# Three edits at the end of a routed-expert kernel: scatters declared free of each other, the last tile's last two weight groups block by block, its last rows scaled by one operation

## The chip, the cores and the metric

The kernel runs on one core of one Trainium2 chip. The metric is the device time of one execution in microseconds. Engines are named as in the profile: PE is the matrix engine (PEld its weight loads), DVE the vector engine, ACT the scalar engine, POOL the GpSimd engine, SP the engine that issues most transfers. A trailing q (POOLq, SPq) marks rows of the engine's instruction queue: waits on semaphores, branches, register loads, drains.

## The reference, cut to what matters

Three layers follow each other. First a decaying linear attention (2 batches, 8 heads, 768 positions), whose output is laid out as 1536 tokens of 512 values. Then a dense two-layer network (512 to 2048 to 512) over all tokens. Then a mixture of 8 experts, of which each token uses one:

```python
expert_idx = np.argmax(logits, axis=1)
...
gate_w = probs[np.arange(N), expert_idx]
out = np.zeros((N, D), dtype=np.float32)
for e in range(E):
    mask = expert_idx == e
    h = np.maximum(x[mask] @ w1[e], 0.0)
    out[mask] = gate_w[mask, None] * (h @ w2[e])
```

Each of the 1536 rows of the result belongs to one token, hence to one expert, and is written once.

## The kernel before, in words

The dense layer and the experts are one list of `units`, one for each weight group. 24 units are the dense layer's (three chunks of four 128-token blocks, eight groups each). 16 units are the experts': four tiles of `WIDTH` 512, 384, 384 and 272 tokens, four groups each. Each tile holds tokens of one expert, chosen at run time. Tokens that don't fit go through a loop at the end (`tc.For_i`), which makes no pass with the inputs used here: each engine loads the loop's limit (L1050), branches past it (L1051), and meets the other engines in the closing rows, which carry L1126.

A tile (`Tile2`) is worked through like this. `gather` fetches its rows from a buffer in HBM and `gather_gate` the gates, by indirect transfers that POOL issues. `xprep` turns the rows. Then, for each group g, `l1` computes 256 hidden values for all tokens of the tile (24 matmuls), ACT and DVE write them as a rounded part `mh` and a remainder `ml`, and `l2` adds their product with the second weights to one accumulator for each block of 128 tokens: six matmuls for a block. In g = 3, the last group, `l2` also ends the block: ACT scales the accumulator by the gates into `osb` (L828), and POOL issues an indirect transfer that scatters these rows to the result `out` (L829). Blocks of a tile are numbered j; the last tile (272 tokens) has blocks of 128, 128 and 16.

The unit loop runs one unit ahead with `l1`: at step n it issues `l1` of unit n, and then `l2` of unit n-1 for all blocks. After the loop, `l2` of the last unit runs for all blocks. So PE's order at the end is: `l1` of the last unit, the last but one's `l2` for j = 0, 1, 2, the last one's `l2` for j = 0, 1, 2. The order on PE is the order of the program text. On the other engines a scheduler orders the instructions of the program and adds the waits that their data need; two scatters to `out` go to rows known at run time only, and the scheduler takes them as writes to the same tensor, one after the other.

For the last block of the last tile (16 tokens) the scaling is split by columns between ACT (L825) and DVE (L826). `osb` has four buffers.

Of the kernel before, what the change touches and what calls it, by code (L numbers as in the profile page):

```python
# [13 lines left out]
AF = mybir.ActivationFunctionType  # L14
ALU = mybir.AluOpType
# [3 lines left out]
NTOK = 1536  # L19
# [8 lines left out]
WIDTH = (512, 384, 384, 272)  # L28
QUARTERS = (4, 3, 3, 3)
NT = len(WIDTH)  # L30
ACC0 = (0, 0, 3, 2)
# [16 lines left out]
def kernel(  # L48
# [15 lines left out]
    V, A, G, PE, SP = nc.vector, nc.scalar, nc.gpsimd, nc.tensor, nc.sync  # L64
# [121 lines left out]
    NU = len(units)  # L186
# [561 lines left out]


    class Tile2:  # L750
        def __init__(self, e, ix, row, gx, gates, nt, nrow=NTOK, acc0=0, end=False):
            self.e, self.ix, self.row, self.gx, self.gates = e, ix, row, gx, gates
            self.nt, self.nrow, self.acc0, self.end = nt, nrow, acc0, end
            self.widths = [min(P, nt - P * j) for j in range((nt + P - 1) // P)]
            self.nb = len(self.widths)

# [51 lines left out]
        def l2(self, n, g, j):  # L808
            hi, lo = (x.rearrange("p (f d) -> p f d", f=2) for x in parts[2, n])
            gh, gl = act[n]  # L810
            w = self.widths[j]
            if g == 0:
                acc[self, j] = ps_acc.tile([P, DM], F32, name="m2a", tag=f"acc{(self.acc0 + j) % 4}")
            a = acc[self, j][0:w, :]
            sl = slice(j * P, j * P + w)
            for f in range(2):
                PE.matmul(a, lhsT=gh[:, f, sl], rhs=hi[:, f, :], start=(g == 0 and f == 0), stop=False)  # L817
                PE.matmul(a, lhsT=gh[:, f, sl], rhs=lo[:, f, :], start=False, stop=False)  # L818
                PE.matmul(a, lhsT=gl[:, f, sl], rhs=hi[:, f, :], start=False, stop=(g == 3 and f == 1))  # L819
            if g == 3:  # L820
                o = sb4.tile([P, DM], F32, name="osb", tag="x2s")
                gate = self.gate[0:w, j:j + 1]
                if self.end and j == self.nb - 1:

                    A.activation(o[0:w, 0:256], a[:, 0:256], AF.Copy, scale=gate)  # L825
                    V.tensor_scalar(o[0:w, 256:512], a[:, 256:512], gate, None, op0=ALU.mult)  # L826
                else:
                    A.activation(o[0:w, :], a, AF.Copy, scale=gate)  # L828
                G.indirect_dma_start(  # L829
                    out=out, out_offset=bass.IndirectOffsetOnAxis(ap=self.row[0:w, j:j + 1], axis=0),  # L830
                    in_=o[0:w, :], in_offset=None, bounds_check=NTOK - 1, oob_is_err=False,
                )


    at_tags.extend(([(ps_acc, f"acc{i}") for i in range(4)] + [(ps_at, "at")] * 2) * (NSTART + 1))
# [46 lines left out]
    def at(step, *fs):  # L882

        s0 = round(4 * step)
        for i, f in enumerate(fs):
            if f:
                plan.setdefault(s0 + i, []).append(f)
# [26 lines left out]
    def chunk_routed(c):  # L914
        rt["cnt"] = route_a(c)
        if first_blk[c] + CHUNKS[c] == EARLY:
            at(now[0] + 1.0, early_tile())
        if c == len(CHUNKS) - 1:
            ei, rt["next"] = route_next(rt["cnt"])
            e = SP.value_load(ei[0:1, 0:1], min_val=0, max_val=NE - 1)  # L920
            ix = small([P, QUARTERS[1]], "ixn", I32)
            tiles.append(Tile2(e, ix, None, None, gate_f, WIDTH[1], acc0=ACC0[1]))
            row_gates(EARLY, NBLK)
            A.dma_start(out=gate_f.rearrange("(p m) o -> p (m o)", m=NBLK), in_=gts)
            eis, rt["others"] = route_rest()
            rt["es"] = eis
# [8 lines left out]
    def other_rows():  # L935
        n = rt["rest"] + 2 * TMAX
        pt = rt["others"]()
        ix = small([P, n], "ixr", I32)
        V.tensor_copy(ix, pt)
        last = rt["rest"] - 1  # L940
        V.tensor_scalar(ix[:, last:last + 1], pt[:, last:last + 1], rt["fit"][:, 0:1], None, op0=ALU.mult)
        row, gx = places(ix, n, NBLK, "r")
        rt["tables"] = tuple(x[:, rt["rest"]:] for x in (ix, row, gx))
        c0 = 0
        for t in range(2, NT):
            e = SP.value_load(rt["es"][t - 2][0:1, 0:1], min_val=0, max_val=NE - 1)
            sl = slice(c0, c0 + QUARTERS[t])
            tiles.append(Tile2(e, ix[:, sl], row[:, sl], gx[:, sl], gate_f, WIDTH[t], acc0=ACC0[t], end=(t == NT - 1)))
            c0 += QUARTERS[t]

    def m2_l2(n, j):
        _, t, g = units[n]
        tiles[t].l2(n, g, j)
        if j == tiles[t].nb - 1:
            parts.pop((2, n))
            act.pop(n)

    for n in range(NU):
        lay, c, g = units[n]
        if lay == 1 and g == 0:  # L960
            if c + 1 < len(CHUNKS):
                m0 = first_blk[c + 1]
                fs = [f for m in range(max(m0, NSTART), m0 + CHUNKS[c + 1]) for f in pcs[m]]
                spread(fs, n + SPREAD[0], n + SPREAD[1])
            if c == 1:
                setup_routing()
        load_w(1, n + 2)
        load_w(2, n + 1)
        if n > K0:
            with tc.issue_after(last.ins):  # L970
                prep_w(1, n + 1)
                prep_w(2, n)
        else:
            with ExitStack() as after:
                if n == 0:

                    after.enter_context(tc.issue_after(ast[CHUNKS[0] - 1, "xl"].ins))
                    after.enter_context(tc.issue_after(whi[1, 0].ins))
                elif n == 1:
                    after.enter_context(tc.issue_after(squared[0, 1].ins))  # L980
                prep_w(1, n + 1)
                if n:
                    prep_w(2, n)
        if lay == 1:
            for f in range(2):
                done = m1_l1(n, f)
                if n == 0 and f == 1:

                    with tc.issue_after(done.ins), tc.issue_after(squared[0, 1].ins):
                        prep_w(2, 0)  # L990
                place(n, f)
                if n == N1 - 1:
                    tiles[0].xprep(2 * f)
                    tiles[0].xprep(2 * f + 1)
        else:
            if n == N1:

                last_scores = [m1_l2(n - 1, j) for j in range(CHUNKS[-1])]
            after_f = {
                N1: (((1, 0), (2, 0), (0, 0)), ((1, 1), (3, 0), (0, 1))),  # L1000
                N1 + 1: (((2, 1), (1, 2)), ((3, 1), (2, 2))),
            }.get(n, ((), ()))
            for f in range(2):
                last = tiles[c].l1(n, f)
                for m, i in after_f[f]:
                    last_scores[m][i]()
                if n == N1 + 2 and f == 1:
                    next_rows()
                if n == N1 + 3 and f == 0:
                    other_rows()  # L1010
                if c and c + 1 < NT and g == 0 and f == 0:
                    tiles[c + 1].gather()
                    tiles[c + 1].gather_gate()
                if c == 0 and g == 3:
                    tiles[1].xprep(2 * f)
                    tiles[1].xprep(2 * f + 1)
                if c and c + 1 < NT and g >= 2:
                    tiles[c + 1].xprep(2 * (g - 2) + f)
        if n == 0:
            place(0, 2)  # L1020
            place(0, 3)
        if n >= 1:
            lay1, c1, g1 = units[n - 1]
            if lay1 == 1 and n < N1:
                pend = []
                for j in range(CHUNKS[c1]):
                    pend.append(m1_l2(n - 1, j))
                    if j % 2 == 1:
                        place(n, 2 + j // 2)
                if g1 == 7:  # L1030
                    for j, p_ in enumerate(pend):
                        at(n + 1 + X2STEP[c1] * j, lambda p_=p_: [f() for f in p_])
                    at(n + ROUTE[c1], lambda c=c1: chunk_routed(c))
            elif lay1 == 2:
                for j in range(tiles[c1].nb):
                    m2_l2(n - 1, j)
                    if n == N1 + 1 and j == 0:
                        last_scores[3][2]()
                    if n == N1 + 1 and j == 2:
                        chunk_routed(len(CHUNKS) - 1)  # L1040
    for j in range(tiles[-1].nb):
        m2_l2(NU - 1, j)

    assert not plan

# [85 lines left out]
```

## Time and profile before

| what | us |
|---|---|
| median of 3 runs | 480.46 (479.46 to 480.70) |
| the profiled execution's own time | 479.74 |
| its span in the trace | 477.9 |
| PE busy in the span | 464.0 (97%) |
| the end of the last matmul's row | 466.56 |

The span runs from the first to the last instruction in the trace; the profiled execution's own time holds 1.8 us more. Tables of windows give, for each stretch, the busy time of each engine with the number of instructions, then the granted share of PE's clock, the share of the DMA engines that was busy, and the GB/s moved.

### The profile page before, as it was taken

The numbers are of one execution on the slowest core, as the hardware profiler recorded it, in microseconds if no ns is written. First come the engines' busy times: TensorE is split into PE (matmuls) and PEld (weight loads), VectorE is DVE, ScalarE is ACT, GpSimd is POOL, SyncE is SP. The second block draws the span as 40 slices with busy tenths as digits, with TensorE's granted clock in tenths as the row PEclk, the third lists the DMA queues.
The fourth block names the chain that finished last, engine by engine and source line by source line (L and its number), as shares of the span: only waits on it lengthen the run. The fifth ranks groups of instructions, "written<-read, shape, count | busy, mean of one in ns | idle before, by whom it ended". The sixth has DMA issues, their size and how long they took to land. (4 is left out here: it accounts for less than half of the span.)

```text
span 477.9 us, 7360 instructions
## 1 busy us (share of the span) xinstructions
PE 464.0 (97%) x2713; PEld 377.7 (79%) x2713; DVE 328.0 (69%) x726; ACT 266.7 (56%) x403; POOL 81.3 (17%) x83
## 2 busy tenths in 40 slices
PE   8999999999999999999999999999999999999990
PEld 5875778878878787878888888887878998998870
DVE  6889979879399997464999785666874354444410
ACT  2388879868975455445756754667233435435320
POOL 4513210002003120000000007000164400400201
PEclk9999999999999999999999999999999999999996
DMA  8999987768564223221433235330456543543201
GB/s 336 423 408 375 394 310 254 291 243 253 195 218 171 95 89 133 87 84 64 163 123 98 89 100 188 104 138 1 175 179 197 177 162 103 188 141 111 87 1 48
DMA packets 22651, 83.65 MB, mean 175 GB/s; under 512 B 3595, under 2 KB 3595, under 8 KB 20564
## 3 DMA queue, kind: packets, MB, share of 16 engines
q1 hardware_dynamic: 15842, 65.04, 38.9%
q10 hardware_dynamic: 4322, 11.55, 6.2%
q0 software_dynamic: 2448, 6.56, 3.9%
q8 instruction: 22, 0.36, 0.3%
q14 instruction: 17, 0.14, 0.1%
HBM read 68.44 MB, written 14.73 MB: 174 GB/s over the span
## 5 line engine op out<-in xcount | busy, mean ns | idle before, releaser
L213 DVE TENSOR_TENSOR w2l<-rw,w2h 128x1024 fp32r<-128x1024 f32 x32 | 39.2, 1225 | 55.2 <-ACT w2h L212 55.1
L700 PE MATMUL l<-xh,w1h 128*128 128x512 f32 x192 | 75.3, 397 | 0.9 <-ACT w1h L212 0.6
L743 PE MATMUL acc<-w2h,gh 128*128 128x512 f32 x184 | 72.8, 396 | 0.0
L702 PE MATMUL l<-xl,w1h 128*128 128x512 f32 x184 | 71.7, 390 | 0.0
L703 PE MATMUL l<-xh,w1l 128*128 128x512 f32 x184 | 71.7, 390 | 0.0
L745 PE MATMUL acc<-w2h,gl 128*128 128x512 f32 x184 | 71.7, 390 | 0.0
L744 PE MATMUL acc<-w2l,gh 128*128 128x512 f32 x184 | 71.7, 389 | 0.0
L212 ACT ACTIVATE w2h<-rw 128x1024 fp32r<-128x1024 f32 x32 | 33.9, 1059 | 57.1 <-PE m2a L819 30.0
L449 DVE CUSTOM_DVE_ANT_0 jk<-x2s,enb 128x512 f32<-128x512 f32 x72 | 48.0, 699 | 0.8 <-ACT x2s L434 0.6
L726 ACT ACTIVATE gh<-g_t 128x512 fp32r<-128x512 f32 x46 | 28.9, 629 | 33.0 <-DVE g_t L722 33.0
L213 DVE TENSOR_TENSOR w1l<-rw,w1h 128x1024 fp32r<-128x1024 f32 x32 | 39.7, 1241 | 11.1 <-ACT w1h L212 10.2
L719 ACT ACTIVATE r_t<-l,half 128x512 f32<-128x512 f32 x48 | 32.4, 680 | 26.2 <-PE l L703 25.8
L794 PE MATMUL m<-x2h,w1h 128*128 128x384 f32 (+2 forms) x128 | 43.9, 343 | 0.0
L700 PEld LDWEIGHTS l<-xh,w1h 128*128 128x128 f32 x192 | 35.8, 188 | 10.1 <-ACT w1h L212 1.2
L796 PE MATMUL m<-x2h,w1l 128*128 128x384 f32 (+2 forms) x128 | 43.3, 338 | 0.0
L795 PE MATMUL m<-x2l,w1h 128*128 128x384 f32 (+2 forms) x128 | 43.1, 337 | 0.0
L722 DVE SCALAR_TENSOR_TENSOR g_t<-r_t,l 128x512 f32<-128x512 f32 x46 | 31.4, 682 | 16.1 <-ACT r_t L720 16.0
L817 PE MATMUL m2a<-w2h,mh 128*128 128x512 f32 (+1 forms) x104 | 41.5, 399 | 0.0
L819 PE MATMUL m2a<-w2h,ml 128*128 128x512 f32 (+1 forms) x104 | 40.8, 392 | 0.0
L743 PEld LDWEIGHTS acc<-w2h,gh 128*128 128x128 f32 x184 | 34.5, 188 | 7.8 <-issue 0.5
L818 PE MATMUL m2a<-w2l,mh 128*128 128x512 f32 (+1 forms) x104 | 40.7, 391 | 0.0
L703 PEld LDWEIGHTS l<-xh,w1l 128*128 128x128 f32 x184 | 34.6, 188 | 7.2
(252 smaller groups left out, 843.9 us busy)
## 6 DMA issues: line engine op xcount, KB each, us to landing
rw<-wsc SPq DMA_DIRECT2D x32, 512.0 KB, 3.4
rw<-in_w_dram SPq DMA_DIRECT2D x32, 512.0 KB, 3.9
rw<-in_w_in_dram SPq DMA_DIRECT2D x8, 1024.0 KB
rw<-in_w_out_dram SPq DMA_DIRECT2D x8, 1024.0 KB, 12.8
wsc<-cw ACTq DMA_DIRECT2D x15, 512.0 KB, 6.8
qk_t<-in_qk_dram SPq DMA_DIRECT2D x12, 512.0 KB, 5.3
kv_t<-in_kv_dram SPq DMA_DIRECT2D x12, 512.0 KB, 12.5
x2d<-x2s ACTq DMA_DIRECT2D x12, 256.0 KB, 2.9
```

The costliest lines, as they stand in the source:

```text
L213: wlo[key] = eng.tensor_tensor(lo, r, hi.bitcast(F32), op=ALU.subtract)
L449: V.tensor_tensor_reduce(out=jk, in0=x2s, in1=enb[e // 2][:, e % 2, :], scale=1.0, scalar=0.0, op0=ALU.mult, op1=ALU.add, accum_out=lr[:, ...
L700: PE.matmul(pt, lhsT=hi[:, f, k, :], rhs=xh[c][:, k, :], start=(k == 0), stop=False)
L702: PE.matmul(pt, lhsT=hi[:, f, k, :], rhs=xl[c][:, k, :], start=False, stop=False)
L703: PE.matmul(pt, lhsT=lo[:, f, k, :], rhs=xh[c][:, k, :], start=False, stop=(k == 3))
L743: PE.matmul(a, lhsT=gh[:, f, sl], rhs=hi[:, f, :], start=(g == 0 and f == 0), stop=False)
L744: PE.matmul(a, lhsT=gh[:, f, sl], rhs=lo[:, f, :], start=False, stop=False)
L745: PE.matmul(a, lhsT=gl[:, f, sl], rhs=hi[:, f, :], start=False, stop=(g == 7 and f == 1))
L794: PE.matmul(pt, lhsT=hi[:, f, k, :], rhs=self.xh[:, k, :], start=(k == 0), stop=False)
L795: PE.matmul(pt, lhsT=hi[:, f, k, :], rhs=self.xl[:, k, :], start=False, stop=False)
L796: PE.matmul(pt, lhsT=lo[:, f, k, :], rhs=self.xh[:, k, :], start=False, stop=(k == 3))
L817: PE.matmul(a, lhsT=gh[:, f, sl], rhs=hi[:, f, :], start=(g == 0 and f == 0), stop=False)
```

## The change

Three things change, all in how the experts' results are finished.

1. Each scatter to `out` is put into one group, `rows_out`, and declared to have no dependency on the others in it.
2. At the last step of the unit loop, `l2` of the last two units runs block by block: unit NU-2 and unit NU-1 for j = 0, then both for j = 1, then both for j = 2. The loop behind it that ran the last unit is gone. `used` now releases the weights and activations of a unit.
3. The last block's 16 rows are scaled by one ACT operation over 512 columns, as those of all other blocks; the parameter `end` goes.

```diff
-    def __init__(self, e, ix, row, gx, gates, nt, nrow=NTOK, acc0=0, end=False):
+    def __init__(self, e, ix, row, gx, gates, nt, nrow=NTOK, acc0=0):
...
             if g == 3:
                 o = sb4.tile([P, DM], F32, name="osb", tag="x2s")
-                gate = self.gate[0:w, j:j + 1]
-                if self.end and j == self.nb - 1:
-
-                    A.activation(o[0:w, 0:256], a[:, 0:256], AF.Copy, scale=gate)
-                    V.tensor_scalar(o[0:w, 256:512], a[:, 256:512], gate, None, op0=ALU.mult)
-                else:
-                    A.activation(o[0:w, :], a, AF.Copy, scale=gate)
-                G.indirect_dma_start(
+                A.activation(o[0:w, :], a, AF.Copy, scale=self.gate[0:w, j:j + 1])
+                rows_out = G.indirect_dma_start(
                     out=out, out_offset=bass.IndirectOffsetOnAxis(ap=self.row[0:w, j:j + 1], axis=0),
                     in_=o[0:w, :], in_offset=None, bounds_check=NTOK - 1, oob_is_err=False,
                 )
+
+                tc.add_to_no_dep_group("rows_out", rows_out.ins)
+                tc.declare_no_dep(rows_out.ins, group="rows_out", reason="no two slots hold the same row")
...
     def m2_l2(n, j):
         _, t, g = units[n]
         tiles[t].l2(n, g, j)
-        if j == tiles[t].nb - 1:
-            parts.pop((2, n))
-            act.pop(n)
+
+    def used(n):
+        parts.pop((2, n))
+        act.pop(n)
...
+            elif n == NU - 1:
+
+                nb = tiles[c1].nb
+                for j in range(nb):
+                    m2_l2(n - 1, j)
+                    m2_l2(n, j)
+                used(n - 1)
+                used(n)
             elif lay1 == 2:
                 for j in range(tiles[c1].nb):
                     m2_l2(n - 1, j)
...
-    for j in range(tiles[-1].nb):
-        m2_l2(NU - 1, j)
+                used(n - 1)
```

## Rows read from the trace of the kernel before

**Rows 1.** The page's busy time, share of the span and instruction count of each engine

```profile
PE 464.0 (97%) x2713; PEld 377.7 (79%) x2713; DVE 328.0 (69%) x726; ACT 266.7 (56%) x403; POOL 81.3 (17%) x83
```

**Rows 2.** Busy time by stage: the experts' tiles, the last matmuls, and what follows them

```profile
core 0: us, PE busy (x) PEld busy (x) DVE busy (x) ACT busy (x) POOL busy (x), PEclk, DMA share, GB/s
...
400.00:462.00 62.00, 62.00 (x345) 54.18 (x344) 25.89 (x34) 25.13 (x39) 10.45 (x9) 1.00 0.34 111
462.00:466.56 4.56, 4.56 (x20) 2.81 (x18) 0.00 (x0) 1.38 (x2) 0.99 (x1) 1.00 0.07 27
466.56:477.94 11.38, 0.00 (x0) 0.00 (x0) 0.47 (x1) 0.47 (x1) 1.85 (x2) 0.58 0.11 41
```

**Rows 3.** Timeline from 462 us: start, duration, instruction, then idle before it and releaser

```profile
463.38 0.39 PE L819 MATMUL m2a<-w2h,ml 128*128 128x512 f32 x1
...
463.81 0.69 ACT L828 ACTIVATE osb<-m2a,gate 128x512 f32<-128x512 f32 x1 [5.16 <-PE m2a L819]
...
464.77 0.99 POOL L829 DMA_INDIRECT out_dram<-osb,rowr  x1 [14.64 <-ACT osb L828]
...
465.21 0.69 ACT L828 ACTIVATE osb<-m2a,gate 128x512 f32<-128x512 f32 x1 [0.71 <-PE m2a L819]
...
466.16 0.40 PE L819 MATMUL m2a<-w2h,ml 128*16 128x512 f32 x1
466.60 0.47 ACT L825 ACTIVATE osb<-m2a,gate 16x256 f32<-16x256 f32 x1 [0.70 <-PE m2a L819]
467.10 0.47 DVE L826 TENSOR_SCALAR osb<-m2a,gate 16x256 f32<-16x256 f32 x1 [7.97 <-ACT osb L825]
468.23 0.98 POOL L829 DMA_INDIRECT out_dram<-osb,rowr  x1 [2.47 <-ACTq L1051]
471.75 0.87 POOL L829 DMA_INDIRECT out_dram<-osb,rowr  x1 [2.54 <-issue]
```

**Rows 4.** Line 829 on POOL and its queue, 467 to 469 us: duration min/median/max

```profile
L829 POOLq EVENT_SEMAPHORE  x2: 2885/2895/2905, 464.6 to 468.1; - x2
```

**Rows 5.** Busy time in the microseconds in which the scatters' data move

```profile
466.00:467.00 1.00, 0.56 (x3) 0.03 (x1) 0.00 (x0) 0.40 (x1) 0.00 (x0) 1.00 0.64 262
469.00:470.00 1.00, 0.00 (x0) 0.00 (x0) 0.00 (x0) 0.00 (x0) 0.21 (x1) 0.50 0.23 94
470.00:471.00 1.00, 0.00 (x0) 0.00 (x0) 0.00 (x0) 0.00 (x0) 0.00 (x0) 0.50 0.42 168
473.00:474.00 1.00, 0.00 (x0) 0.00 (x0) 0.00 (x0) 0.00 (x0) 0.00 (x0) 0.50 0.13 31
```

**Rows 6.** Lines 1051 and 1126, the branch past the loop and the closing rows

```profile
L1051 POOLq INC_SWDGE_SEM  x1: 978/978/978, 472.5 to 472.5; - x1
...
L1126 POOLq DRAIN  x1: 3252/3252/3252, 473.5 to 473.5; - x1
...
L1126 SPq EVENT_SEMAPHORE  x2: 28/28/28, 473.9 to 474.0; - x2
```

**Rows 7.** Timeline of PE, ACT and DVE, 456 to 461 us

```profile
456.32 1.22 DVE L213 TENSOR_TENSOR w2l<-rw,w2h 128x1024 fp32r<-128x1024 f32 x1 [4.38 <-ACT w2h L212]
...
458.05 0.40 PE L817 MATMUL m2a<-w2h,mh 128*128 128x512 f32 x1
...
458.25 0.40 ACT L802 ACTIVATE mh<-m 128x272 fp32r<-128x272 f32 x1 [1.12 <-PE m L796]
...
458.68 0.44 DVE L803 SCALAR_TENSOR_TENSOR ml<-m,mh 128x272 fp32r<-128x272 f32 x1 [0.78 <-ACT mh L802]
...
459.67 0.40 PE L818 MATMUL m2a<-w2l,mh 128*128 128x512 f32 x1
...
460.60 0.40 PE L819 MATMUL m2a<-w2h,ml 128*128 128x512 f32 x1
```

**Rows 8.** Timeline of POOL, 355 to 360 us: gathers issued one behind the other

```profile
355.53 0.95 POOL L763 DMA_INDIRECT xg<-x2d,ixr  x1 [0.31 <-issue]
356.79 0.95 POOL L763 DMA_INDIRECT xg<-x2d,ixr  x1 [0.30 <-issue]
358.04 1.48 POOL L763 DMA_INDIRECT xg<-x2d,ixr  x1 [0.30 <-issue]
```

**Rows 9.** Waits from 300 us on: total us, times, longest

```profile
ACT w2h L212 <- PE m2a L819: 30.0, 10, 4.5
...
ACT osb L828 <- PE m2a L819: 10.6, 9, 5.2
```

More of the change, by code (lines that the diff above doesn't have):

```diff
@@ L750 @@
     class Tile2:
-        def __init__(self, e, ix, row, gx, gates, nt, nrow=NTOK, acc0=0, end=False):
+        def __init__(self, e, ix, row, gx, gates, nt, nrow=NTOK, acc0=0):
             self.e, self.ix, self.row, self.gx, self.gates = e, ix, row, gx, gates
-            self.nt, self.nrow, self.acc0, self.end = nt, nrow, acc0, end
+            self.nt, self.nrow, self.acc0 = nt, nrow, acc0
             self.widths = [min(P, nt - P * j) for j in range((nt + P - 1) // P)]
@@ L947, in other_rows @@
             sl = slice(c0, c0 + QUARTERS[t])
-            tiles.append(Tile2(e, ix[:, sl], row[:, sl], gx[:, sl], gate_f, WIDTH[t], acc0=ACC0[t], end=(t == NT - 1)))
+            tiles.append(Tile2(e, ix[:, sl], row[:, sl], gx[:, sl], gate_f, WIDTH[t], acc0=ACC0[t]))
             c0 += QUARTERS[t]
```

## The prediction, as made before the result

> **What bounds the kernel now.** I first read the page's busy times: PE works 464.0 us of the span, 97% [rows 1]. That says that the body is PE's and that a gain elsewhere must come from a stretch in which PE does nothing. The table by stage finds it [rows 2]: PE is busy 62.00 of 62.00 us from 400 to 462, 4.56 of 4.56 to the end of its last row at 466.56, and then 11.38 us follow in which no engine but POOL does more than half a microsecond. The timeline of the end shows what these are [rows 3]. The three scatters of the last tile start on POOL at 464.77, 468.23 and 471.75, though the rows of the second are scaled by 465.21 + 0.69 = 465.90 and those of the third by 467.10 + 0.47 = 467.57. The queue rows of the scatter line say why [rows 4]: two semaphore waits of 2.885 and 2.905 us begin at 464.6 and 468.1, so they end at 467.5 and 471.0, each some 0.75 us before the next scatter starts. The data of the scatters move between: 262 GB/s in the microsecond from 466, 94 and 168 in the two from 469 [rows 5]. So each scatter waits until the one before has landed. The names of releasers in [rows 3] (a branch on ACT's queue, "issue") are no help here: what is late is the landing.
>
> From the last scatter the end follows at a fixed distance. POOL runs an instruction of 0.978 us at 472.5 and a drain of 3.252 us at 473.5 that ends at about 476.79; SP's wait for the last landing is over by 473.9, and the span ends at 477.94 [rows 2, 6]. From the third scatter's start to the end that is 477.94 - 471.75 = 6.19 us.
>
> **The change, part by part.** The time is set by the third scatter's start plus 6.19, so each edit is priced by what it does to that start.
>
> *Scatters free of each other.* Nothing holds a scatter then but its own rows and POOL itself. The first scatter shows the step from rows to issue: ACT ends at 463.81 + 0.69 = 464.50, POOL starts at 464.77, 0.27 later [rows 3]. POOL itself can issue such transfers about 1.26 us apart: gathers without a wait between them stand 1.26 and 1.25 us apart, 0.30 idle [rows 8]. With the order on PE and the split as they are, the second scatter would start at 465.90 + 0.27 = 466.17 (POOL is free at 464.77 + 0.99 + 0.30 = 466.06), the third at 467.57 + 0.27 = 467.84: 3.91 us earlier than 471.75. This edit alone is nearly the whole gain.
>
> *The last two groups block by block.* No matmul is added or taken away. 36 matmuls run from 458.05 in steps of 0.23, six to a block and unit. Now block 0 ends with the 24th (row at 463.38), block 1 with the 30th, block 2 with the 36th (466.16). After the change block 0 ends with the 12th (the row at 460.60), block 1 with the 24th, block 2 with the 36th as before [rows 3, 7]. ACT starts the scaling 0.04 us after the last matmul's row ends, so block 0's `osb` is ready at 461.04 + 0.69 = 461.73 and its scatter starts at 462.00; block 1's takes block 0's present place, 464.77; block 2's is unchanged. With the waits gone, this edit is worth nothing in the end: block 2 still ends last. With the waits left in, it would be worth much (rival A). What it asks for earlier is the last unit's data: `w2l` in the eighth matmul (the row at 459.67) rather than the 20th, and it is ready at 456.32 + 1.22 = 457.54; the second half of `ml` in the 12th (460.60), and it is ready at 458.68 + 0.44 = 459.12 [rows 7]. Margins of 2.1 and 1.5 us hide it; if a margin were gone, PE would idle for what is missing, and the end would move by as much.
>
> *One operation for the last rows.* The two halves don't run side by side: DVE starts at 467.10, ACT ended at 467.07, and DVE's row names ACT as its releaser [rows 3]. One ACT operation of 16x512 isn't in the trace; it lies between 16x256 (0.47) and 128x512 (0.69). It has the columns of the second and the rows of the first. I take 0.69: with 16 rows half the columns still cost 0.47, so the rows aren't what ACT saves on, and the columns are those of the row of 0.69. Then `osb` is ready at 466.60 + 0.69 = 467.29 instead of 467.57, 0.28 earlier; at 0.47 it would be 0.50 earlier. Before the change this was hidden under the wait to 471.0; with the waits gone it counts in full.
> The Trainium skill ("ScalarE: Activation LUTs", What ACT_TABLE_LOAD costs) gives 186 ns and 0.833 ns a column, and 93 ns for each pointer operand, whatever the rows: an estimate of 0.71 us for 512 columns with the gate as pointer, which would make the gain 4.17 rather than 4.19. The row of 0.69 bears that out for 128 partitions; no row shows 16.
>
> *Sum.* The third scatter starts at 466.60 + 0.69 + 0.27 = 467.56; POOL has been free since 464.77 + 0.99 = 465.76. That is 4.19 us before 471.75. The three scatters then stand 2.78 and 2.79 apart, while the data of one move within about a microsecond [rows 5], so they don't meet.
>
> *The other ten scatters.* Those of the first three tiles are freed too, and the scheduler may place them and the gathers among them otherwise on POOL. Nothing on the path waits for them: in [rows 9] ACT's `osb` waits for PE's accumulator, not for a free buffer, and ACT's weight conversion waits for PE, not for a transfer; PE has no gap in 400 to 462. I cost them at nothing, hidden under PE. If that cover is gone, rival C says what it costs.
>
> **The numbers.** The span becomes 477.94 - 4.19 = 473.75, the profiled execution's own time 479.74 - 4.19 = 475.55, and the median 480.46 - 4.19 = 476.27, which I forecast as 476.3. The profiled execution lies 0.72 below the median of the runs.
>
> **The rivals.** *A. The waits stay.* The declaration may not take effect, or a wait on a reused semaphore may take the old one's place. Then the order on PE does the work: scatter 0 starts at 462.00, lands 2.73 later (464.77 to 467.5) at 464.73, scatter 1 starts 0.73 after that, 465.46, lands 2.77 later at 468.23, scatter 2 starts 0.75 later at 468.98. Gain 2.77, time 477.7. For it: only that the scheduler places the waits. Against it: gathers, which have nothing to wait for, show no such wait [rows 8].
>
> *B. Completions are served one after the other.* POOL's drain ends 2.89 us after SP saw the last landing (476.79 against 473.9) [rows 6]. If POOL spends that time on each transfer in turn, then scatter 0 (landed 464.73) is done at 467.62, scatter 1 (467.50) at 470.51, scatter 2 (467.56 + 2.15 = 469.71) at 473.40, and the end follows 1.15 later at 474.55. Gain 3.39, time 477.1. For it: nothing else in the rows explains a drain of 3.25 us. Against it: the present end fits a fixed distance just as well.
>
> *C. The scheduler's new order costs PE.* If in the first three tiles, with ten block ends, ACT's queue now takes an `osb` (0.69) ahead of an activation that PE waits for, each costs up to 0.69; four of them eat 2.8 and leave a gain of 1.4 or less. Against it: `osb` already waits for PE and has no reason to move; only POOL loses waits. Time about 479.1 to 480.5, no measurable change.
>
> *D. The other side: the drain pays for each scatter.* If the waits between scatters were where POOL finished the last transfer, and the drain now finishes all three, it costs 3 x 3.25 instead of 3.25. It would start 4.19 earlier, at 469.35, end at 479.10, and the span at 480.25: 2.31 longer, time 482.8. It decides once each added piece is over 2.1 us. Against it: between landing (467.5) and the next start (468.23) POOL needs only 0.73, and gathers in a row start 1.26 apart with no such block between them [rows 8]. For it: the row of an indirect transfer is short (0.87) beside the drain that follows.
> On that row the Trainium skill ("Perfetto Trace Analysis", DMA Instruction — SWDGE (GPSIMD)) says that the profiler's end is when the last descriptor is written, and that the core completes the instruction later; so hidden work on POOL behind the row is possible, and no row here shows how much.
>
> **Chances.** The forecast 0.74, A 0.07, B 0.08, C 0.06, D 0.05. About 0.3% (1.4 us) is what a measurement of this kernel can tell from no change. Forecast, A and B are faster: 0.89; C is the same: 0.06; D is slower: 0.05. The range runs from the lowest run less the gain, 479.46 - 4.19 = 475.3, less 0.2 for the cheaper ACT operation, 475.1, to A's 477.7 with 0.2 for the runs above their median, 477.9; it takes in B.
>
> **What the next profile should show.** Scatters of the last tile at about 462.0, 464.8 and 467.6, no semaphore wait of 2.9 us on POOL's queue in that stretch, one `osb` row of about 0.69 at 466.6 and none on DVE, PE's last row still ending at 466.56, a drain of about 3.25 from 469.3, and an end at 473.75. The prediction is wrong if PE's last row moves (order or readiness), if the scatters still stand 3.5 us apart (A), or if the drain is longer (B, D).

## The result, and the profile after

| | before | after |
|---|---|---|
| median us | 479.96 (479.33 to 480.70, 4 runs) | 475.23 (474.53 to 475.31, 4 runs) |
| ratio, 95% interval | | 0.9894 [0.9875, 0.9914] |
| span of the profiled execution | 477.94 | 472.65 |
| from the end of PE's last row to the end of the span | 11.38 | 6.28 |

The kernel is faster by 1.1%, about 5 us; 4.2 us were forecast. The interval of the timed runs is 4.1 to 6.0 us, so they alone don't rule out 4.2; it is the traces below that do. The table by stage of the changed kernel answers to [rows 2]. Its last stretch begins where PE's last row ends.

```profile
core 0: us, PE busy (x) PEld busy (x) DVE busy (x) ACT busy (x) POOL busy (x), PEclk, DMA share, GB/s
400.00:462.00 62.00, 62.00 (x344) 54.73 (x343) 25.67 (x34) 25.81 (x40) 9.87 (x10) 1.00 0.32 111
462.00:466.37 4.37, 4.37 (x19) 2.08 (x17) 0.00 (x0) 0.69 (x1) 1.77 (x2) 1.00 0.22 88
466.37:472.65 6.28, 0.00 (x1) 0.00 (x0) 0.00 (x0) 0.68 (x1) 0.87 (x1) 0.69 0.09 32
```

PE is as full as before, and only the stretch behind it shrank, from 11.38 to 6.28 us. The timeline of the end of the changed kernel answers to [rows 3] and [rows 7].

```profile
460.41 0.40 PE L819 MATMUL m2a<-w2h,ml 128*128 128x512 f32 x1
...
460.85 0.69 ACT L822 ACTIVATE osb<-m2a,gate 128x512 f32<-128x512 f32 x1 [2.39 <-PE m2a L819]
...
461.81 0.98 POOL L823 DMA_INDIRECT out_dram<-osb,rowr  x1 [19.17 <-ACT osb L822]
...
463.63 0.69 ACT L822 ACTIVATE osb<-m2a,gate 128x512 f32<-128x512 f32 x1 [2.10 <-PE m2a L819]
...
464.59 0.98 POOL L823 DMA_INDIRECT out_dram<-osb,rowr  x1 [1.80 <-ACT osb L822]
...
465.97 0.40 PE L819 MATMUL m2a<-w2h,ml 128*16 128x512 f32 x1
466.41 0.68 ACT L822 ACTIVATE osb<-m2a,gate 16x512 f32<-16x512 f32 x1 [2.09 <-PE m2a L819]
467.36 0.87 POOL L823 DMA_INDIRECT out_dram<-osb,rowr  x1 [1.79 <-ACT osb L822]
```

Each scatter now names ACT's `osb` as its releaser, starts 0.27 us after it, and stands 2.8 us from the next. The third starts 0.99 us after PE's last row (467.36 - 466.37); 1.00 was forecast. So far the steps held. The end is the surprise: 472.65 - 467.36 = 5.29 us behind the third scatter, where I had put 6.19. These are the rows of POOL's queue for the branch past the loop (L1056) and the closing drain (L1131), which answer to [rows 6]; start times are at the end of each row.

```profile
L1056 POOLq INC_SWDGE_SEM  x1: 951/951/951, 465.3 to 465.3; - x1
...
L1131 POOLq DRAIN  x1: 4363/4363/4363, 467.1 to 467.1; - x1
...
L823 POOLq MOVE  x2: 29/29/29, 461.6 to 466.3; - x2
```

The 0.95 us instruction of the branch, which stood behind the third scatter before (472.5 against 471.75), now runs at 465.3, two us ahead of it. The drain begins before the scatter does and ends at 471.5. The last row shown has the register moves of two scatters: the later one, at 466.3, is the third scatter's, and it stands right behind the branch's instruction, which ends at 466.29. The order of POOL's instructions in the program of the changed kernel says how that came about (its last rows, loop body left out; the row marked ISA is the 0.95 us instruction):

```
48 L823 DMA out_dram<-osb,rowr 1536x512 x5
49 L1055 TENSOR_LOAD lim
50 L1056 COMPARE_AND_BRANCH
...
63 L1056 ISA
64 L1056 UNCONDITIONAL_BRANCH
65 L823 DMA out_dram<-osb,rowr 1536x512
```

Before, all six scatters of the last two tiles stand ahead of the branch. Now five do, and the sixth, the last block's, stands behind the loop and its branch.

### The profile page after: what moved, and what is told of

It reads as the page before. It is cut to its first block, busy times and chain, and to the rows that moved or that the text cites. A ratio compares the mean times of both kernels' runs of the same rounds, so it can differ in the third digit from the quotient of the medians.

```text
span 472.7 us, 7356 instructions
## 1 busy us (share of the span) xinstructions
PE 463.7 (98%) x2713; PEld 377.7 (80%) x2713; DVE 326.7 (69%) x725; ACT 266.6 (56%) x403; POOL 82.4 (17%) x83
## 4 chain that ended last, share of the span: by engine, by line
PE 68%; issue 20%; POOL 6%; DVE 3%; ACT 1%; POOLq 0%; another core or an unknown queue 0%; ACTq 0%
PE l L700 10%; PE acc L743 9%; PE l L702 9%; PE acc L744 9%; PE l L703 9%; PE acc L745 9%; POOL out_dram L823 2%; PE ao L335 2%; PE sc L308 2%; POOL xg L763 2%; POOL gate L771 2%; PE acc L738 1%; PE ao L348 1%; PE as L377 1%; PE m L794 1%
## 5 line engine op out<-in xcount | busy, mean ns | idle before, releaser
L745 PEld LDWEIGHTS acc<-w2h,gl 128*128 128x128 f32 x184 | 34.5, 188 | 7.3
```

## The experiments

Two numbers of each trace are compared: the third scatter's start after the end of PE's last row, and the end of the span after that start. Their sum is free of what PE's part does from one execution to the next, which the last experiment shows to be more than some of the differences. Each line is one profiled execution. The page of the profile calls spans on POOL rough; the sum does not depend on them, the split into two columns does.

| run | third scatter after PE | end after it | sum | timed ratio, 95% |
|---|---|---|---|---|
| before | 5.19 | 6.19 | 11.38 | |
| one operation alone | 5.19 | 6.18 | 11.37 | 1.0002 [0.9982, 1.0023] |
| block order alone | 2.53 | 6.19 | 8.72 | 0.9943 [0.9926, 0.9961] |
| free alone | 2.41 | 5.29 | 7.70 | 0.9936 [0.9911, 0.9961] |
| free, one operation | 2.41 | 5.29 | 7.71 | 0.9914 [0.9892, 0.9935] |
| free but for the loop's, one operation | 0.99 | 6.44 | 7.43 | 0.9925 [0.9906, 0.9944] |
| changed, loop's scatters not free | 0.99 | 6.28 | 7.27 | 0.9906 [0.9884, 0.9927] |
| changed, memset behind | 0.99 | 5.95 | 6.94 | 0.9910 [0.9875, 0.9945] |
| free, block order | 1.28 | 5.30 | 6.58 | 0.9903 [0.9877, 0.9928] |
| changed | 0.99 | 5.29 | 6.28 | 0.9892 [0.9869, 0.9915] |

The line of the changed kernel is that of its second profile. The timed ratios have intervals of 0.8 to 1.7 us to each side; differences below that are read from the traces alone.

**The changed kernel again.** No edit.

> The changed kernel itself, again, as the measure for the three beside it. Theory P (POOL's order): because the loop's scatters are in the group too, the scheduler could put the last tile's third scatter behind the loop's branch on POOL, so that the branch and the 0.95 us instruction behind it run while POOL waits for rows; the time from the third scatter's start to the end of the span is then 5.3 us in place of 6.2. Theory L (landing): the order does not matter, the end follows the last landing or the rest of the earlier transfers' handling, which is shorter here by chance or because the scatters overlap. Both expect here what was measured once: about 4.7 to 5.1 us less than before, third scatter 1.28 us after the end of PE's last row minus 0.3, so about 1.0 us after it, and 5.3 us from there to the end.

Measured: 474.80 against 479.80 us; 0.99 and 5.29 us, as the first time. (The text's "1.28 minus 0.3" and "1.0" are the same figure, 0.99 here.)

**The changed kernel with the loop's scatters outside the group.** This decides between the two theories of the shorter tail.

```diff
+                if self.nt == 2 * P:
+                    return
                 tc.add_to_no_dep_group("rows_out", rows_out.ins)
                 tc.declare_no_dep(rows_out.ins, group="rows_out", reason="no two slots hold the same row")
```

(Only the loop's tiles have 2 x 128 tokens.)

> The changed kernel, but the two scatters in the loop (which makes no pass) are left out of the group, so the third scatter must stay ahead of the branch on POOL. Everything else is as in the changed kernel. Theory P: the 0.95 us instruction stands between the third scatter and the drain again, the tail is 6.2 us, and the time is 0.9 us longer than the changed kernel's. Theory L: the tail stays at 5.3 us and the time is the changed kernel's.

In the program's order all six scatters stand ahead of the branch again. The third scatter, the stretch behind PE's last row, and the rows of the branch (L1058) and the drain (L1133) on POOL's queue in this run:

```profile
466.93 0.87 POOL L823 DMA_INDIRECT out_dram<-osb,rowr  x1 [1.78 <-ACT osb L822]
...
465.94:473.21 7.27, 0.00 (x1) 0.00 (x0) 0.00 (x0) 0.68 (x1) 0.87 (x1) 0.68 0.08 28
...
L1058 POOLq INC_SWDGE_SEM  x1: 969/969/969, 467.7 to 467.7; - x1
...
L1133 POOLq DRAIN  x1: 3386/3386/3386, 469.0 to 469.0; - x1
```

The third scatter starts at 466.93, the instruction runs behind it, and the end comes 6.28 us after it instead of 5.29. The third scatter landed 2.15 us after its start in both runs (469.08 here, 469.51 in the changed kernel), so the landing does not account for the 0.99 us. Theory P holds, theory L falls. The pieces of the 6.28 are not quite those of the old 6.19: the drain ends 3.74 us after the branch's instruction, 3.28 before, and the span ends 0.82 us after the drain, 1.15 before; why stays open. The two timed ratios (0.9892 and 0.9906) lie in that order, but their intervals overlap.

**Scatters free, nothing else.**

```diff
-                G.indirect_dma_start(
+                rows_out = G.indirect_dma_start(
...
+                tc.add_to_no_dep_group("rows_out", rows_out.ins)
+                tc.declare_no_dep(rows_out.ins, group="rows_out", reason="no two slots hold the same row")
```

> The kernel before with the scatters declared free and nothing else: order on PE and split of the last rows as before. By my terms the third scatter starts 467.84 - 466.56 = 1.28 us after PE's last row ends, 3.91 us earlier than before. Theory P: the third scatter goes behind the branch here too, so the tail is 5.3 us and the gain is 3.91 + 0.91 = 4.8 us (ratio 0.990). Theory L without the new order of blocks: the three scatters stand 1.3 to 1.7 us apart, their handling overlaps, and the tail is 6.2 us or longer: gain 3.9 us or less (ratio 0.992).

The tail is 5.29, as theory P said. But the third scatter starts 2.41 us after PE's last row, not 1.28, and the gain is 3.68 us in the trace, near theory L's number for another reason. POOL's timeline and, from its queue, the row of the branch (L1054) and the third scatter's register move:

```profile
464.64 0.98 POOL L829 DMA_INDIRECT out_dram<-osb,rowr  x1 [21.95 <-ACT osb L828]
466.04 0.98 POOL L829 DMA_INDIRECT out_dram<-osb,rowr  x1 [0.42 <-ACT osb L828]
468.84 0.87 POOL L829 DMA_INDIRECT out_dram<-osb,rowr  x1 [1.81 <-DMA gate<-gate_f,gxr]
```

```profile
L1054 POOLq INC_SWDGE_SEM  x1: 951/951/951, 467.0 to 467.0; - x1
...
L829 POOLq MOVE  x1: 29/29/29, 468.0 to 468.0; - x1
```

The branch's instruction runs from 467.0 to 467.95, between the second and the third scatter, and the third, whose queue rows follow at 468.0, starts 0.89 after it; what fills the 0.89 us is not shown. The releaser that the row names, a gate's transfer, had landed long before; it is not what was late.

**Scatters free, one operation, old order on PE.** The edit above, and `end` never set.

> Scatters declared free and the last rows scaled by one operation, the order of blocks on PE as before. By my terms the block order adds nothing once the waits are gone: the same time as the changed kernel within 0.2 us, third scatter 1.0 us after PE's last row. If instead the spacing of the scatters counts (2.8 us apart in the changed kernel, 1.4 here), the tail here is longer than the changed kernel's 5.3 us by up to 1.4.

```profile
468.58 0.87 POOL L829 DMA_INDIRECT out_dram<-osb,rowr  x1 [1.82 <-DMA gate<-gate_f,gxr]
...
466.16:473.87 7.71, 0.01 (x1) 0.00 (x0) 0.00 (x0) 0.68 (x1) 1.47 (x2) 0.75 0.16 60
```

Measured 2.41 and 5.29: the rows were ready about 0.3 us earlier than in the run before and it changed nothing, so the rows aren't what the third scatter waits for. My first reading, that the block order adds nothing, is refuted: against the changed kernel it is worth 7.71 - 6.28 = 1.43 us in the traces (the timed intervals overlap).

**The same with the loop's scatters outside the group.** Both edits from above.

> Scatters declared free except the two in the loop, one operation for the last rows, the order of blocks on PE as before. In the run without the new block order the third scatter started 2.41 us after PE's last row, not 1.0. Theory P2: what held it was the branch with its 0.95 us instruction, now ahead of it on POOL right behind the second scatter. With the branch behind the third scatter again it must start 1.0 us after PE's last row, with a tail of 6.2 to 6.3, 7.3 us together, and be 0.4 us faster than with the branch ahead. Rival R2: scatters 1.4 us apart hold each other up (POOL or the transfers). Then the third starts at 2.4 us here too, and with the tail of 6.2 it ends 8.7 us after PE's last row.

ACT's and POOL's rows of this run, and the branch's (L1056):

```profile
468.86 0.68 ACT L828 ACTIVATE osb<-m2a,gate 16x512 f32<-16x512 f32 x1 [0.70 <-PE m2a L819]
```

```profile
467.03 0.98 POOL L829 DMA_INDIRECT out_dram<-osb,rowr  x1 [21.95 <-ACT osb L828]
468.43 0.98 POOL L829 DMA_INDIRECT out_dram<-osb,rowr  x1 [0.42 <-ACT osb L828]
469.81 0.87 POOL L829 DMA_INDIRECT out_dram<-osb,rowr  x1 [0.40 <-ACT osb L828]
...
L1056 POOLq INC_SWDGE_SEM  x1: 969/969/969, 470.7 to 470.7; - x1
```

With the branch behind it the third scatter starts 0.27 us after its rows again, though the scatters stand only 1.40 and 1.38 us apart. So P2 holds and R2 falls: what held the third scatter was the branch, not the spacing. What follows PE is 7.43 us against 7.71, somewhat less than the 0.4 expected, because the tail is 6.44 here. It is 0.16 us longer than with the scatters 2.8 us apart (6.28): the branch's instruction starts 0.91 us after the third scatter in place of 0.75, while the drain takes 3.39 us in both. So the spacing is not quite free, and why stays open. The timed ratios don't tell the two apart.

**Block order alone.** The edits of the unit loop and `used`, without the others.

> The kernel before with the last two weight groups block by block and nothing else; the scatters wait for each other. By rival A's terms: scatters 4.56 and 1.10 us before and 2.42 us after the end of PE's last row, 2.77 us earlier than before for the third, branch behind the third scatter, tail 6.2 us. Time about 2.8 us less than before (ratio 0.994). If the early use of the last unit's data made PE wait, PE's last row would end later instead.

```profile
461.33 0.98 POOL L829 DMA_INDIRECT out_dram<-osb,rowr  x1 [10.78 <-ACT osb L828]
464.90 0.98 POOL L829 DMA_INDIRECT out_dram<-osb,rowr  x1 [2.59 <-issue]
468.42 0.87 POOL L829 DMA_INDIRECT out_dram<-osb,rowr  x1 [2.54 <-DVEq L1059]
```

The first scatter starts as early as expected (4.56 before the end of PE's last row at 465.89), then each waits for the one before, 3.57 and 3.52 us apart. The gain is 11.38 - 8.72 = 2.66 us, 2.77 expected, and the tail is the old 6.19. PE's order has no wait in it: PE is busy without a gap from 360 to 465.89.

**One operation alone.** `end` never set.

> The kernel before with the last rows scaled by one ACT operation and nothing else. My term: the rows are ready 0.28 us earlier, but the third scatter waits for the second's landing some 4 us longer, so nothing is gained: third scatter 5.2 us after PE's last row, tail 6.2, ratio 1.000. If the wait were not the landing but the rows, the third scatter would start 0.28 us earlier.

Measured 5.19 and 6.18: hidden, as expected.

**Free and block order, split kept.**

> The changed kernel with the last rows split between ACT and DVE as before. My term for the one operation was 0.28 us: third scatter 1.27 us after PE's last row instead of 0.99, tail 5.3, 6.6 us together. If POOL's branch bounds the third scatter here as well, the split costs nothing and the sum is 6.3.

Measured 1.28 and 5.30, sum 6.58: the one operation is worth 0.30 us once nothing else holds the scatter.

**A memset behind the third scatter in the changed kernel.** It clears the attention's mask, which nothing reads by then.

```diff
+    rows_last = []
...
+                rows_last.append(rows_out)
...
+    with tc.issue_after(rows_last[-1].ins):
+        G.memset(dmask, 0.0)
```

> The changed kernel with one added memset of 128x1024 on POOL behind the third scatter (it clears a mask that nothing reads any more). Theory T1: the drain on POOL ends a fixed 3.26 us after POOL's last piece of work, so the end moves by about the memset's duration. Theory T2: the drain follows the last transfer (2.0 us after its landing in the changed kernel), and the memset runs in its shadow: no change if the memset takes less than 3 us.

```profile
467.51 0.87 POOL L824 DMA_INDIRECT out_dram<-osb,rowr  x1 [1.79 <-ACT osb L823]
468.36 0.99 POOL L1054 MEMSET dmask<- 128x1024 f32 x1
```

```profile
L1136 POOLq DRAIN  x1: 5167/5167/5167, 467.5 to 467.5; - x1
```

The drain ends at 472.63, 3.28 us after the memset's end at 469.35; in the changed kernel it ends 3.26 after the scatter's row (468.23), and before 3.28 after the 0.98 us instruction. T2 falls: the drain ends 2.96 us after the last landing (469.67), not 2.0. So T1 holds for the drain. The end of the span moved by 5.95 - 5.29 = 0.66 us, not the memset's 0.99: from the drain's end to the span's it took 0.83 us here and 1.17 in the changed kernel. The difference lies right behind the drain: the queue's next row starts 0.04 us after it here (472.67) and 0.38 us after it in the changed kernel (471.87). Why stays open.

**The kernel before, once more.**

> The kernel before, profiled once more, to see how far the end of PE's last row moves from one execution to the next without any change. Runs of the changed kernel and its variants ended PE between 465.9 and 466.7 us. If that is scatter between executions, this run falls anywhere in or about that range and what follows PE's last row takes 11.4 us as before. If the change itself had shortened PE's part, this run repeats 466.56.

PE's last row ended at 466.39 without any change, 0.17 earlier than in the first profile, and what follows took 11.36 us:

```profile
466.39:477.75 11.36, 0.00 (x1) 0.00 (x0) 0.47 (x1) 0.47 (x1) 1.85 (x2) 0.59 0.10 40
```

The 0.19 us by which the changed kernel's PE ended earlier than in the first profile is thus about what two executions of the kernel before differ by, and needs no effect of the change. In the run with one operation alone it ended at 468.63, in the one with free scatters but for the loop's, one operation and the old order at 468.82.

## Why the prediction was right in sign and short in size

**What held.** The bound was read rightly: PE full to its last row, then a chain of scatters each waiting for the last one's landing. The waits are gone, the scatters start at 461.81, 464.59 and 467.36 (forecast 462.0, 464.8, 467.6), each 0.27 us after its rows. (The 2.78 between the first two is 2.77 by the prediction's own terms.) One ACT operation of 16x512 takes 0.68 us (0.69 taken), so 16 rows cost here what 128 do; before the change no row could show it. The early use of the last unit's data cost PE nothing. The ten other scatters cost nothing: PE is busy 45.00 of 45.00 us from 355 to 400, before and after, and 62.00 of 62.00 from 400 to 462.

**The step that failed** is "From the last scatter the end follows at a fixed distance", 6.19 us. It measured 5.29. The 0.98 us instruction in that distance belongs to the branch past the loop, and I took its place behind the last scatter for given; the prediction allowed for a new order on POOL only among the other ten scatters. But the group also holds the loop's two scatters. With that dependency gone, nothing kept the last scatter ahead of the loop, and the scheduler put it behind; the branch now runs while POOL waits for the rows. Before, its instruction ended 0.88 us after the last scatter's row (473.50 against 472.62); that is what fell away. The run with the loop's scatters outside the group shows it: the branch is behind again, and the distance is 6.28. The other runs agree. Without the memset there are eleven profiles: in the six with the branch behind the third scatter the distance is 6.18 to 6.44 us, in the five with it ahead 5.29 or 5.30. In the two profiled executions the gain of 477.94 - 472.65 = 5.29 us is 4.20 from the earlier third scatter (4.19 forecast), 0.90 of this, and 0.19 of PE's part, which changed by 0.17 without any edit. The forecast of a gain of 4.2 against the 5.1 of the traces (11.38 - 6.28) is short by that term.

**A second step was wrong without touching the sum:** "With the waits gone, this edit is worth nothing in the end." That is true only while the branch stays behind (there it is worth 7.43 - 7.27 = 0.16 us). With the branch ahead of the third scatter, the old order leaves it no free place: the second scatter starts 1.40 us after the first, the branch follows, and the third is held until 2.41 us after PE. The new order moves the second scatter from 0.4 to 1.8 us before PE's end, the branch fits between, and that is worth 1.43 us. So the term "this edit alone is nearly the whole gain" was wrong too: free alone gives 3.68 us of the 5.10 (3.91 by my terms), where a later third scatter (2.41 for 1.28) eats what the shorter tail gives.

**The rivals.** A (the waits stay) is refuted by the rows of the scatters. The order alone, A's case, came within 0.11 us of its price. B and D put the drain's length down to the scatters' handling in turn. Neither came: with the branch ahead, scatters 1.4 us apart leave the same tail of 5.29 as scatters 2.8 us apart; with it behind, the tails differ by 0.16 but the drain takes 3.39 us in both. With the branch ahead the drain ends 3.26 us after the last scatter's row. My reading of the long drain as work per transfer had no support. The Trainium skill ("Perfetto Trace Analysis", DMA Instruction — SWDGE (GPSIMD)) states that the core completes the instruction after the row's end. The 3.26 us between the row's end and the drain's allow for such work, but a memset is followed by the same 3.28, so these runs don't show it. C (new order costs PE) did not come; the scheduler's new order did come, on POOL and in the kernel's favour.

No version tried here beats the changed kernel in the traces; the timed intervals of the nearest overlap with its own. What is left behind PE is 6.28 us: 0.99 to the scatter, 0.87 for it, 3.26 of drain, 1.17 to the end.

## What to carry to other kernels

To drop a dependency is to change what the scheduler may reorder. List every instruction that the dropped edge pinned, those behind a branch and those in loops that make no pass included, and ask what the queue holds between the freed instruction and the end. And price edits as a set: here the block order was worth 2.66 us alone, 0.16 or 1.43 beside the freed scatters depending on where the branch stood.

Where PE's part varies by more than the effect, measure from PE's last row to the end; it repeated within 0.02 us over the executions of both kernels (11.38 and 11.36; 6.28 and 6.28), while whole runs of the kernel before spread from 479.0 to 482.6 us.

## What the runs showed of the hardware

POOL's closing drain ended 3.26 to 3.28 us after POOL's last piece of work where that was a scatter, a memset, or, in the kernel before, the branch's instruction. In the two runs with the loop's scatters outside the group it was 3.74 (in the changed kernel's variant from 467.68 + 0.97 to 469.00 + 3.39); why stays open. A scatter behind the branch's instruction started 0.89 us after that instruction's end in the two runs in which it was held by it. The names of releasers on POOL were of little use: for scatters that waited for a landing the rows named a branch on another engine or "issue", and for one that waited for POOL itself a gate's transfer of long before.
